# Loading one expert's weights piece by piece behind the streamed pieces, and the table rows later, at the seam of a fused three-layer kernel

## The chip, the cores and the metric

The kernel runs on one core of one Trainium2 chip. The metric is the device time of one execution in microseconds, and lower is better. Before the change, three runs took 1038.91 to 1043.51 us, with a median of 1040.13 us.

## What is computed

Three layers follow one another. The first is attention over 4 x 8 heads of 576 tokens, in which each row keeps its 32 largest scores. The second is a dense layer on 2304 tokens of width 512: `h = x @ w_in`, a gate, `@ w_out` (hidden width 2048). The third sends each token to one of 8 experts:

```python
logits = xn @ en.T / tau
expert_idx = np.argmax(logits, axis=1)
...
for e in range(E):
    mask = expert_idx == e
    h = np.maximum(x[mask] @ w1[e], 0.0)
    out[mask] = gate_w[mask, None] * (h @ w2[e])
```

`w1[e]` is 512 x 1024 and `w2[e]` 1024 x 512, both 2 MB. All is in 32-bit floats; a product is made of three matmuls on a high and a low part of each factor (high x high, high x low, low x high).

## The kernel before

Five engines work from lists of their own, in the order in which the program names their instructions: PE (matmuls and transposes), DVE and ACT (vector and scalar work), POOL (vector work and the indirect DMAs), and SP, which issues the plain DMAs. The order is written out by hand, and each engine keeps it: an instruction that waits holds back all that stand behind it on its engine.

The tokens come in groups of 128. Attention hands pairs of groups to the dense layer, which works in 8 steps (`q`, here also `n`) per pair. A step has a first half (`s1`, 24 matmuls of 256 columns, line 602) and a second half (`s2`, 12 matmuls of 512 columns, line 637), and the second half of a step runs after the first half of the next one. The high parts of the dense weights stay on the chip. The low parts are written to DRAM once and streamed back for every pair, one piece of 512 KB (`lo`) per half step; each of the two streams has two buffers, so SP can issue a piece when the half step two before has freed its buffer (line 286).

The last pair of groups (16 and 17, `finals`) has nothing left to overlap with but the third layer, and the seam between them is where the change lies. The function `behind(n, k)` is called four times in each of the last 8 steps, `k` = 0 in the middle of the first half, 1 after it, 2 and 3 after each part of the second half. It places these things there:
- `place()` writes the rows of a group's tokens into a table in DRAM (`tbl`), sorted by expert, by an indirect DMA on POOL (line 729).
- `expert(r)` reads the number of the expert with rank `r` (by size) into a register of SP (line 801). `load_ids` reads that expert's rows of the table (`idt`, line 806), `get` gathers up to 128 token rows (`xg`) by them on POOL (line 976), and `turn_in` transposes a block of them on PE (line 987) and splits it into a high and a low part on ACT and DVE.
- `load1` and `load2` load an expert's `w1` and `w2` in four pieces of 512 KB each (lines 811 and 820); `split_1` and `split_2` make the high part of a piece on ACT (line 824) and the low part on DVE (line 825).

After the loop the two final groups are scored: transposed, multiplied with the experts' embeddings (lines 1105 and 1114), their experts chosen on DVE (`choose`), ranked (`rank`: two small matmuls on PE, then positions on DVE) and placed. The rows of the table that belong to blocks 2 and 3 of the first expert can be read only then. Around these stand the first expert's own matmuls on its blocks 0 and 1 (`hidden`, line 917; `second`, line 951). From then on the eight experts follow one another, and each one's weights and rows are loaded while the one before is computed. `TURNS` is the order of the experts. The experts with rank 0 and 1 are called the first and the next expert below.

Of the kernel before, what the change touches and what calls it, by code (L numbers as in the profile page):

```python
# [20 lines left out]
DM, FF = 512, 2048  # L21
# [72 lines left out]
def layers(tc: tile.TileContext, qt, kt, v, w_in, w_out, embt, tau, w1, w2, out, y_dram, g_dram, tbl, lo_dram, flag, pools, consts):  # L94
# [704 lines left out]
    def expert(r):  # L799
        if r not in evs:  # L800
            evs[r] = nc.values_load(ordi[0:1, r:r + 1], engines=[ET.SP], min_val=0, max_val=E - 1)
            idts[r] = late["ids"].tile([128, 4, 2], I32, name=f"idt{r}")

    def load_ids(r, b0, b1):
        expert(r)
        nc.sync.dma_start(out=idts[r][:, b0:b1, :], in_=tbl[bass.ds(evs[r] * STRIDE + 128 * b0, 128 * (b1 - b0)), :].rearrange("(n p) t -> p n t", p=128))

    def load1(r):
        t = late["w1" if r == 0 else "wb"].tile([128, 4, F2], F32, tag="raw", name="a1")
        for k in range(4):  # L810
            nc.sync.dma_start(out=t[:, k, :], in_=w1r[:, bass.ds(evs[r], 1), k, :].rearrange("p o f -> p (o f)"))
        ws1[r] = t

    w2r = w2.rearrange("e (k p) d -> p e k d", p=128)
    ws2 = {}

    def load2(r):
        t = late["w1"].tile([128, 8, DM], F32, tag="raw", name="a2")
        for k in range(0, 8, 2):
            nc.sync.dma_start(out=t[:, k:k + 2, :], in_=w2r[:, bass.ds(evs[r], 1), k:k + 2, :].rearrange("p o k d -> p (o k) d"))  # L820
        ws2[r] = t

    def split(hi, lo, x):
        nc.scalar.copy(hi, x)  # L824
# [64 lines left out]
    if True:  # L889
# [17 lines left out]
        def hidden(r, f, c0, c1, half=None):  # L907
            xh_, xl_ = tok[r]
            h1, l1 = ws1[r]
            if r not in hs:  # L910
                hs[r] = [hp.tile([128, 8, CAPS[0]], F32R, tag=t, name=t) for t in ("hh", "hl")]
            if half != 1:
                xt_[f] = late["ph"].tile([128, 512], F32, tag="ph", name="ph2")[:, :c1 - c0]
            ph = xt_[f]
            for k in ((0, 1), (2, 3), (0, 1, 2, 3))[2 if half is None else half]:
                for n, (l, x) in enumerate(((h1, xh_), (h1, xl_), (l1, xh_))):
                    nc.tensor.matmul(ph, l[:, k, 128 * f:128 * f + 128], x[:, k, c0:c1], start=(k == 0 and n == 0), stop=(k == 3 and n == 2))

        def hidden_out(r, f, c0, c1):
            hh, hl = hs[r]  # L920
            ph = xt_.pop(f)
            nc.scalar.activation(hh[:, f, c0:c1], ph, AF.Relu)  # L922
            nc.vector.scalar_tensor_tensor(hl[:, f, c0:c1], ph, 0.0, hh[:, f, c0:c1].bitcast(F32), op0=ALU.max, op1=ALU.subtract)  # L923
# [18 lines left out]
        def second(r, b, fs_):  # L942
            hh, hl = hs[r]
            h2, l2 = ws2[r]
            n, o, m = b
            if (r, n) not in sums_:
                sums_[r, n] = po_.tile([128, DM], F32, tag="po", name="po2")
            po = sums_[r, n]
            for f in fs_:
                for i, (a, w) in enumerate(((hh, h2), (hl, h2), (hh, l2))):  # L950
                    nc.tensor.matmul(po[:m, :], a[:, f, o:o + m], w[:, f, :], start=(f == 0 and i == 0), stop=(f == 7 and i == 2))
# [21 lines left out]
        def get(r, b):  # L973
            n, o, m = b
            xg_[r, n] = xg = late["xg"].tile([128, DM], F32, tag="xg", name="xg")
            nc.gpsimd.indirect_dma_start(out=xg[:m, :], out_offset=None, in_=y_dram,
                                         in_offset=bass.IndirectOffsetOnAxis(ap=idts[r][:m, n, 0:1], axis=0))
# [13 lines left out]
        def split_1(r, k):  # L991
            if k == 0:
                ws1[r] = (ws1[r], [late["w1"].tile([128, 4, F2], F32R, tag=t, name=t) for t in ("h1", "l1")])
            a1, (h1, l1) = ws1[r]
            split(h1[:, k, :], l1[:, k, :], a1[:, k, :])
            if k == 3:
                ws1[r] = (h1, l1)

        def split_2(r, k):
            if k == 0:  # L1000
                ws2[r] = (ws2[r], [wb.tile([128, 8, DM], F32R, tag=t, name=t, bufs=2) for t in ("h2", "l2")])
            a2, (h2, l2) = ws2[r]
            split(h2[:, 2 * k:2 * k + 2, :], l2[:, 2 * k:2 * k + 2, :], a2[:, 2 * k:2 * k + 2, :])
            if k == 3:
                ws2[r] = (h2, l2)

        def gate_part(k):
            if k == 0:
                for t, g in finals:
                    sq = gp.tile([128, DM], F32, tag="ob", name="sql")  # L1010
                    nc.scalar.activation(sq, t, AF.Square, accum_out=ss_all[:, g:g + 1])
            elif k == 1:
                late["nrm"] = nrm = fs.tile([128, NG], F32, tag="nrm", name="nrm")
                nc.scalar.activation(nrm, ss_all, AF.Sqrt)
                nc.vector.tensor_scalar(nrm, nrm, 1e-6, None, op0=ALU.add)
                nc.vector.reciprocal(nrm, nrm)
                df = late["df"]
                nc.vector.tensor_tensor(df, df, nrm.unsqueeze(2).broadcast_to([128, NG, E]), op=ALU.mult)
                nc.scalar.activation(df, df, AF.Exp)
            elif k == 2:  # L1020
                late["gt"] = gt = fs.tile([128, NG], F32, tag="gt", name="gt")
                nc.vector.tensor_reduce(gt, late["df"], axis=AX.X, op=ALU.add)
                nc.vector.tensor_scalar(gt, gt, 1e-9, None, op0=ALU.add)
                nc.vector.reciprocal(gt, gt)
            else:
                pg = half_a()
                nc.tensor.transpose(pg[:NG, :128], late["gt"], ident)
                gts = fs.tile([NG, 128], F32, tag="df", name="gts")
                nc.vector.tensor_copy(gts, pg[:NG, :128])
                nc.sync.dma_start(out=g_dram[0:NT, :].rearrange("(g p) o -> g (p o)", p=128), in_=gts)  # L1030
# [5 lines left out]
        def behind(n, k):  # L1036
            n -= base
            if (n, k) == (0, 1):
                place()
            elif (n, k) == (0, 3):  # L1040
                side.popleft()()
            elif (n, k) == (1, 0):
                side.popleft()()
            elif (n, k) == (1, 1):
                side.popleft()()
                place()
            elif (n, k) == (1, 3):
                side.popleft()()
                choose()
            elif (n, k) == (2, 0):  # L1050
                rank()
                place()
            elif (n, k) == (2, 1):
                place()
            elif (n, k) == (3, 1):
                expert(0)
                load1(0)
            elif (n, k) == (3, 3):
                load_ids(0, 0, 2)
            elif (n, k) == (4, 0):  # L1060
                for x in bl[0][:2]:
                    get(0, x)
            elif (n, k) == (6, 0):
                turn_in(0, bl[0][0])
            elif (n, k) == (6, 2):
                turn_in(0, bl[0][1])
            elif (n, k) == (6, 3):
                load2(0)
                expert(1)
            if (n, k) in ((4, 1), (4, 3), (5, 1), (5, 3)):  # L1070
                split_1(0, ((4, 1), (4, 3), (5, 1), (5, 3)).index((n, k)))

        with tc.manual_schedule():
            at.close()
# [24 lines left out]
            load1(1)  # L1099
            C = (0, 256)  # L1100
            yts = []
            for o, (t, g) in enumerate(finals):
                pp = px.tile([128, 4, 128], F32, tag="px", name="pxt")
                for k in range(4):
                    nc.tensor.transpose(pp[:, k, :], t[:, 128 * k:128 * k + 128], ident)
                yts.append(gp.tile([128, 4, 128], F32, tag="ob", name="ytl"))
                nc.scalar.copy(yts[o], pp)
                hidden(0, 0, *C, o)
            split_2(0, 0)
            hidden_out(0, 0, *C)  # L1110
            p2 = half_a()
            for o, (t, g) in enumerate(finals):
# [2 lines left out]
                scored[0] += 1  # L1115
            nc.vector.tensor_copy(l_all[:, NG - 2:NG, :], p2[:, :2 * E].rearrange("p (g e) -> p g e", e=E))
            choose()
            hidden(0, 1, *C)
            hidden_out(0, 1, *C)
            hidden(0, 2, *C, 0)  # L1120
            rank()
            place()
# [7 lines left out]
            for f in (3, 4, 5):  # L1130
                split_2(0, f - 2)
                first(0, f, *C)
            load_ids(1, 0, 4)
            load2(1)
            for r in TURNS[2:]:
                load_ids(r, 0, 4)
            for n in (2, 3):
                get(0, bl[0][n])
            gate_part(0)
            for f in (6, 7):  # L1140
                first(0, f, *C)
# [4 lines left out]
            turn_in(0, bl[0][2])  # L1146
            get(1, bl[1][0])
            gate_part(3)
            second(0, bl[0][1], range(4, 7))
            turn_in(0, bl[0][3])  # L1150
            get(1, bl[1][1])
# [136 lines left out]
```

## Time and profile before

| what | before |
|---|---|
| median of three runs | 1040.13 us |
| the profiled execution | 1039.81 us |
| its span, first to last instruction | 1038.0 us |
| TensorE (PE) busy | 956.5 us, 92% |
| VectorE (DVE) busy | 759.7 us, 73% |
| ScalarE (ACT) busy | 712.4 us, 69% |
| GpSimd (POOL) busy | 632.0 us, 61% |
| mean granted clock of TensorE | 0.968 |
| DMA, mean over the span | 174 GB/s |

The profile shows one execution. Times are counted from the span's start; the span leaves out 1.8 us of the execution's own time. "Idle before" is what an engine waited in front of an instruction, with the engine or DMA that ended the wait. The granted clock is a share of TensorE's full 2.4 GHz. Attention ends at about 700 us, the seam lies between 740 and 820 us, and the experts take the rest.

### The profile page before, as it was taken

What the parts mean: (1) busy time and instruction counts of PE and PEld (TensorE: products, weight loads), DVE (VectorE), ACT (ScalarE), POOL (GpSimd) and SP (SyncE); (2) the same over time, 40 slices, a digit from 0 to 9 for tenths busy, and PEclk for the clock granted to TensorE, in tenths of its full rate; (3) what the DMA queues carried; (4) which work ended last, traced back from release to release, by engine and by line L of the source; (5) the groups of instructions that cost most, each with busy time, mean ns of one, the idle gap of its engine ahead of it and who ended that gap; (6) DMA issues with size and microseconds to landing.
All of it is one profiled execution on the core that took longest, in us unless ns stands there. A gap on an engine that the chain in (4) does not pass through costs nothing. (4 is left out here: it accounts for less than half of the span.)

```text
span 1038.0 us, 20808 instructions
## 1 busy us (share of the span) xinstructions
PE 956.5 (92%) x7196; PEld 834.8 (80%) x7196; DVE 759.7 (73%) x2349; ACT 712.4 (69%) x1437; POOL 632.0 (61%) x786
## 2 busy tenths in 40 slices
PE   2666788999999999999999999999989999999997
PEld 1443576889999999999999987889878888888986
DVE  7999999998988988888888888861233454455551
ACT  4899798897788788798787877773334454455551
POOL 4789899877768877678876765763331353223220
PEclk9966799999999999999999999999999999999999
DMA  5555677743455654267564375556684465544620
GB/s 195 178 160 183 220 245 249 230 154 128 133 172 157 201 164 137 88 186 236 127 184 138 101 253 179 157 192 196 170 274 164 127 230 209 203 137 160 236 95 22
DMA packets 85905, 180.96 MB, mean 174 GB/s; under 512 B 16157, under 2 KB 30640, under 8 KB 85791
## 3 DMA queue, kind: packets, MB, share of 16 engines
q1 hardware_dynamic: 81231, 169.68, 50.8%
q0 software_dynamic: 4416, 9.80, 3.0%
q8 instruction: 59, 0.97, 0.4%
q14 instruction: 55, 0.45, 0.1%
q10 hardware_dynamic: 144, 0.07, 0.0%
HBM read 157.41 MB, written 18.89 MB: 170 GB/s over the span
## 5 line engine op out<-in xcount | busy, mean ns | idle before, releaser
L487 POOL TENSOR_TENSOR s<-s,z 128x576 f32<-128x576 f32 x144 | 190.0, 1320 | 63.1 <-ACT z L483 62.5
L602 PE MATMUL bank_h<-xh,vh 128*128 128x256 f32 x576 | 171.4, 298 | 0.0
L602 PE MATMUL bank_h<-xl,vh 128*128 128x256 f32 x576 | 163.7, 284 | 0.0
L602 PE MATMUL bank_h<-xh,lo 128*128 128x256 f32 x576 | 163.5, 284 | 0.0
L469 DVE MAX8 A<-left 128x8 f32<-128x288 f32 (+1 forms) x288 | 159.7, 596 | 0.0
L520 PE MATMUL bank_t<-ident,s 128*128 128x128 f32 x648 | 107.8, 290 | 31.7 <-ACT pt L525 19.7
L525 ACT COPY pt<-bank_t 128x384 f32<-128x384 f32 x216 | 102.1, 481 | 37.0 <-PE bank_t L520 35.9
L520 PEld LDWEIGHTS bank_t<-ident,s 128*128 128x128 f32 x648 | 81.4, 148 | 53.9 <-ACT pt L525 22.8
L621 POOL TENSOR_TENSOR gl<-u,gh 128x512 fp32r<-128x512 f32 x72 | 92.9, 1290 | 47.6 <-ACT gh L618 44.4
L637 PE MATMUL y<-lo,gh 128*128 128x512 f32 x288 | 114.2, 397 | 4.8 <-DMA lo<-lo_dram 4.8
L441 ACT COPY s<-ps_sc 128x576 f32<-128x576 f32 x143 | 92.2, 645 | 38.1 <-PE ps_sc L430 13.9
L637 PE MATMUL y<-wh,gh 128*128 128x512 f32 x288 | 118.2, 410 | 0.0
L483 ACT ACTIVATE z<-s,nb 128x576 bf16<-128x576 f32 x144 | 112.6, 782 | 5.3 <-POOL nb L477 5.3
L637 PE MATMUL y<-wh,gl 128*128 128x512 f32 x288 | 113.8, 395 | 0.0
L493 ACT ACTIVATE s<-s,nb 128x576 f32<-128x576 f32 x144 | 113.4, 788 | 0.5 <-POOL s L487 0.5
L602 PEld LDWEIGHTS bank_h<-xl,vh 128*128 128x128 f32 x576 | 110.8, 192 | 0.3
L602 PEld LDWEIGHTS bank_h<-xh,vh 128*128 128x128 f32 x576 | 110.8, 192 | 0.3
L602 PEld LDWEIGHTS bank_h<-xh,lo 128*128 128x128 f32 x576 | 110.6, 192 | 0.0
L970 POOL DMA_INDIRECT out_dram<-ob,idt x21 | 24.9, 1185 | 139.0 <-ACT ob L963 95.4
L610 ACT ACTIVATE u<-bank_h,half 128x512 f32<-128x512 f32 x72 | 50.0, 694 | 69.2 <-PE bank_h L602 67.7
L825 DVE TENSOR_TENSOR l<-a,h 128x1024 fp32r<-128x1024 f32 x64 | 76.3, 1230 | 26.8 <-ACT h L824 21.8
L923 DVE SCALAR_TENSOR_TENSOR hl<-ph,hh 128x256 fp32r<-128x256 f32 (+5 forms) x72 | 31.7, 440 | 87.2 <-ACT hh L922 85.9
(248 smaller groups left out, 2679.5 us busy)
## 6 DMA issues: line engine op xcount, KB each, us to landing
lo<-lo_dram SPq DMA_DIRECT2D x144, 512.0 KB
a<-in_moe_w_dram SPq DMA_DIRECT2D x64, 512.0 KB
vt<-in_v_dram SPq DMA_DIRECT2D x28, 320.0 KB
w<-in_moe_w_in_dram SPq DMA_DIRECT2D x16, 512.0 KB
w<-in_moe_w_out_dram SPq DMA_DIRECT2D x16, 512.0 KB
lo_dram<-wf SPq DMA_DIRECT2D x32, 256.0 KB
qraw<-in_q_dram SPq DMA_DIRECT2D x48, 128.0 KB
krs<-in_k_dram SPq DMA_DIRECT2D x16, 288.0 KB
```

Source lines behind the costliest of these rows:

```text
L441: nc.scalar.copy(sbuf[i % NS][:, :, HS * g:HS * g + HS], ps_[i][:, :, :HS])
L469: nc.vector.max(A[:, n, 8 * r:8 * r + 8], src[:, n, :w])
L483: nc.scalar.activation(zb_[n], tile_of(i, n), AF.Relu, bias=sel[i][1][:, n, 1:2], scale=-BIG)
L487: nc.gpsimd.tensor_tensor(s, s, zb_[n], op=ALU.subtract)
L493: nc.scalar.activation(s, s, AF.Exp, bias=sel[i][1][:, n, 0:1], scale=SCALE, accum_out=sums[i][:, n:n + 1])
L520: nc.tensor.transpose(pp[:, 128 * k:128 * k + 128], e[:, 128 * (3 * c + k):128 * (3 * c + k) + 128], ident)
L525: nc.scalar.copy(pts[i][:, 3 * c:3 * c + 3, :].rearrange("p k n -> p (k n)"), tb_.pop((i, c))[:, :384])
L602: nc.tensor.matmul(ph[:, a, :], w, x[:, k, :], start=(k == 0 and n == 0), stop=(k == 3 and n == 2))
L610: nc.scalar.activation(u, state[q, "h"], AF.Relu, bias=half, scale=1.0 / 6.0)
L621: nc.gpsimd.tensor_tensor(state[q][1], state.pop((q, "u")).rearrange("p (a n) -> p a n", a=2), state[q][0].bitcast(F32), op=ALU.subtract)
L637: nc.tensor.matmul(state["y"][o], x[:, a, c], w, start=(f == 0 and n == 0), stop=(f == 15 and n == 2))
L825: nc.vector.tensor_tensor(lo, x, hi.bitcast(F32), op=ALU.subtract)
```

## The change

Seven things move; nothing is added or taken away:
- the four pieces of the first expert's `w1`, all issued at step (3, 1), are issued one by one at (3, 3), (4, 1), (4, 3) and (5, 1);
- their splits move from (4, 1), (4, 3), (5, 1), (5, 3) to (4, 3), (5, 1), (5, 3), (6, 1);
- the first two blocks' table rows and gathers move from (3, 3) and (4, 0) to (5, 3), and their `turn_in` from (6, 0) and (6, 2) to (7, 0) and (7, 2);
- the first expert's `w2` moves from (6, 3) to (7, 3);
- after the loop, `hidden` of step 0 stands ahead of the final groups' transposes, and `hidden` of step 1 in the gaps where step 0 stood;
- the first split of `w2` moves from before the choice to after it;
- the gathers of blocks 2 and 3, and the other experts' table rows, come ahead of the next expert's `w2`, which is loaded in two halves.

```diff
-    def load1(r):
-        t = late["w1" if r == 0 else "wb"].tile([128, 4, F2], F32, tag="raw", name="a1")
-        for k in range(4):
-            nc.sync.dma_start(out=t[:, k, :], in_=w1r[:, bass.ds(evs[r], 1), k, :].rearrange("p o f -> p (o f)"))
-        ws1[r] = t
+    raw1, raw2 = {}, {}
+
+    def load1(r, parts=range(4)):
+        if 0 in parts:
+            ws1[r] = raw1[r] = late["w1" if r == 0 else "wb"].tile([128, 4, F2], F32, tag="raw", name="a1")
+        for k in parts:
+            nc.sync.dma_start(out=raw1[r][:, k, :], in_=w1r[:, bass.ds(evs[r], 1), k, :].rearrange("p o f -> p (o f)"))
...
-            elif (n, k) == (3, 1):
-                expert(0)
-                load1(0)
-            elif (n, k) == (3, 3):
+            elif (n, k) == (5, 3):
                 load_ids(0, 0, 2)
-            elif (n, k) == (4, 0):
                 for x in bl[0][:2]:
                     get(0, x)
-            elif (n, k) == (6, 0):
+            elif (n, k) == (7, 0):
                 turn_in(0, bl[0][0])
-            elif (n, k) == (6, 2):
+            elif (n, k) == (7, 2):
                 turn_in(0, bl[0][1])
-            elif (n, k) == (6, 3):
+            elif (n, k) == (7, 3):
+                expert(1)
                 load2(0)
-                expert(1)
-            if (n, k) in ((4, 1), (4, 3), (5, 1), (5, 3)):
-                split_1(0, ((4, 1), (4, 3), (5, 1), (5, 3)).index((n, k)))
+            if (n, k) == (3, 3):
+                expert(0)
+            if (n, k) in PARTS1:
+                load1(0, (PARTS1.index((n, k)),))
+            if (n, k) in SPLITS1:
+                split_1(0, SPLITS1.index((n, k)))
+
+        PARTS1 = ((3, 3), (4, 1), (4, 3), (5, 1))
+        SPLITS1 = ((4, 3), (5, 1), (5, 3), (6, 1))
...
             yts = []
+            hidden(0, 0, *C)
             for o, (t, g) in enumerate(finals):
...
                 nc.scalar.copy(yts[o], pp)
-                hidden(0, 0, *C, o)
-            split_2(0, 0)
+                hidden(0, 1, *C, o)
             hidden_out(0, 0, *C)
...
             choose()
-            hidden(0, 1, *C)
             hidden_out(0, 1, *C)
+            split_2(0, 0)
             hidden(0, 2, *C, 0)
             rank()
...
-            load_ids(1, 0, 4)
-            load2(1)
-            for r in TURNS[2:]:
-                load_ids(r, 0, 4)
             for n in (2, 3):
                 get(0, bl[0][n])
+            for r in TURNS[1:]:
+                load_ids(r, 0, 4)
+            load2(1, (0, 1))
...
             gate_part(3)
+            load2(1, (2, 3))
             second(0, bl[0][1], range(4, 7))
```

`load2` is changed as `load1` is.

On SP, around the first expert's `w1` (tiles: `lo0` and `lo1` the streamed pieces of the two halves, `a1` a weight piece, `idt0` the table rows, `ordi` the expert numbers). Before:

```order
L286 DMA lo0_9788<-lo_dram0_60 128x1024
L801 TENSOR_LOAD ordi_90
...
L811 DMA a1_9808<-in_moe2_w1_dram 128x1024
...
L286 DMA lo1_9825<-lo_dram1_61 128x1024
L806 ISA
L806 DMA idt0_9807<-tbl_59 128x2x2
L286 DMA lo0_9856<-lo_dram0_60 128x1024
L286 DMA lo1_9881<-lo_dram1_61 128x1024
```

The row of `a1` stands there four times, one behind the other. Now:

```order
L286 DMA lo0_9788<-lo_dram0_60 128x1024
L286 DMA lo1_9809<-lo_dram1_61 128x1024
L801 TENSOR_LOAD ordi_90
...
L814 DMA a1_9822<-in_moe2_w1_dram 128x1024
L286 DMA lo0_9848<-lo_dram0_60 128x1024
L814 ISA
L814 DMA a1_9822<-in_moe2_w1_dram 128x1024
L286 DMA lo1_9870<-lo_dram1_61 128x1024
...
L286 DMA lo1_9925<-lo_dram1_61 128x1024
L806 ISA
L806 DMA idt0_9821<-tbl_59 128x2x2
```

The `lo1` piece that stood behind the expert number and all four weight pieces now stands ahead of them, and each `a1` piece has a `lo` piece behind it. The read of the table rows moved behind the last of them.

On DVE, around the choice for the final groups (`l_all` the scores, `picks` the choice, `pos` to `rows` the positions in the table, `l2` the low part of a weight piece, `hl` an expert's hidden values). Before, from the first split of `w2` on:

```order
L825 TENSOR_TENSOR l2_10137<-a2_9997,h2_10136 128x1024
L923 SCALAR_TENSOR_TENSOR hl_10115<-ph2_10116,hh_10114 128x256
L1116 COPY l_all_88<-bank_a_120 128x16
...
L702 TENSOR_TENSOR picks_83<-eqs_10152,first_10155 128x16
L923 SCALAR_TENSOR_TENSOR hl_10115<-ph2_10160,hh_10114 128x256
L714 TENSOR_TENSOR pos_10184<-bank_a_120,ebase_78 128x16
```

Now:

```order
L925 SCALAR_TENSOR_TENSOR hl_10108<-ph2_10109,hh_10107 128x256
L1121 COPY l_all_88<-bank_a_120 128x16
...
L702 TENSOR_TENSOR picks_83<-eqs_10161,first_10164 128x16
L925 SCALAR_TENSOR_TENSOR hl_10108<-ph2_10129,hh_10107 128x256
L827 TENSOR_TENSOR l2_10172<-a2_10053,h2_10171 128x1024
L714 TENSOR_TENSOR pos_10184<-bank_a_120,ebase_78 128x16
```

The subtraction for the first piece of `w2` moved from before the scores' copy to between the choice and the positions.

On SP, behind the table rows of blocks 2 and 3 (`idt1` to `idt5` the other experts' rows, `a2` a piece of the next expert's `w2`). Before:

```order
L806 DMA idt0_9807<-tbl_59 128x2x2
L806 ISA
L806 DMA idt1_10012<-tbl_59 128x4x2
L820 ISA
L820 DMA a2_10255<-in_moe2_w2_dram 128x2x512
...
L801 TENSOR_LOAD ordi_90
L801 ISA x2
L806 ISA
L806 DMA idt2_10270<-tbl_59 128x4x2
```

Now:

```order
L806 DMA idt0_9821<-tbl_59 128x2x2
L806 ISA
L806 DMA idt1_10052<-tbl_59 128x4x2
L801 TENSOR_LOAD ordi_90
L801 ISA x2
L806 ISA
L806 DMA idt2_10269<-tbl_59 128x4x2
...
L806 DMA idt5_10329<-tbl_59 128x4x2
L823 ISA
L823 DMA a2_10331<-in_moe2_w2_dram 128x2x512
```

All four `a2` pieces stood ahead of the six row loads that need an expert number; now the first two stand behind them, and the other two behind the write of the gates.

## Rows read from the trace of the kernel before

**Rows 1.** The page: busy time and share of the span of each engine.
```profile
PE 956.5 (92%) x7196; PEld 834.8 (80%) x7196; DVE 759.7 (73%) x2349; ACT 712.4 (69%) x1437; POOL 632.0 (61%) x786
```

**Rows 2.** Waits of PE, 680 to 1038 us: sum, times, longest.
```profile
PE y L637 <- DMA lo<-lo_dram: 4.4, 2, 3.0
PE pxt L987 <- DMA xg<-y_dram,idt: 1.9, 1, 1.9
...
PE pxt L1105 <- ACT ysl L648: 0.7, 1, 0.7
```

**Rows 3.** Windows: length; busy time of each engine; granted clock, DMA share, GB/s.
```profile
757.30:760.24 2.94, 0.00 (x0) 0.00 (x1) 0.69 (x1) 2.13 (x4) 0.00 (x0) 1.00 0.94 282
760.24:764.45 4.21, 4.21 (x11) 3.34 (x12) 2.36 (x2) 0.92 (x1) 3.49 (x3) 0.59 0.90 330
...
782.21:786.70 4.49, 3.02 (x13) 1.99 (x11) 0.00 (x0) 0.59 (x1) 1.00 (x1) 1.00 0.12 48
...
810.98:813.07 2.09, 0.17 (x1) 0.03 (x1) 0.00 (x0) 0.00 (x0) 0.00 (x0) 1.00 1.14 236
```

**Rows 4.** PE's timeline at the seam: start, duration, line, operation.
```profile
756.89 0.39 PE L637 MATMUL y<-wh,gh 128*128 128x512 f32 x1
...
767.32 0.40 PE L637 MATMUL y<-wh,gh 128*128 128x512 f32 x1
...
770.07 0.28 PE L602 MATMUL bank_h<-xh,vh 128*128 128x256 f32 x1
...
787.53 0.65 PE L1105 MATMUL pxt<-ident,ysl 128*128 128x128 f32 x4 [0.68 <-ACT ysl L648]
...
793.81 0.18 PE L711 MATMUL bank_a<-picks,tri 128*128 128x16 bf16 x1
```

**Rows 5.** SP's timeline at the seam: start and length of issues, line, transfer.
```profile
747.48 2.20 SPq L811 DMA_DIRECT2D a<-in_moe_w_dram  x4
749.78 0.58 SPq L286 DMA_DIRECT2D lo<-lo_dram  x1
756.74 0.38 SPq L806 DMA_DIRECT2D idt<-tbl  x1
...
773.32 3.00 SPq L820 DMA_DIRECT2D a<-in_moe_w_dram  x4
...
801.80 0.97 SPq L806 DMA_DIRECT2D idt<-tbl  x2
803.02 2.08 SPq L820 DMA_DIRECT2D a<-in_moe_w_dram  x4
805.91 9.19 SPq L806 DMA_DIRECT2D idt<-tbl  x6
```

**Rows 6.** DVE's timeline around the choice for the final groups.
```profile
790.94 1.22 DVE L825 TENSOR_TENSOR l<-a,h 128x1024 fp32r<-128x1024 f32 x1 [9.79 <-ACT h L824]
...
792.41 0.17 DVE L1116 COPY l_all<-bank_a 128x16 f32<-128x16 f32 x1
...
794.78 0.17 DVE L718 CAST rows<-de 128x2 int32<-128x2 f32 x1
```

**Rows 7.** POOL's timeline: two gathers, the second with no weights beside it.
```profile
805.20 0.97 POOL L976 DMA_INDIRECT xg<-y_dram,idt  x1 [6.53 <-issue]
...
881.01 1.05 POOL L976 DMA_INDIRECT xg<-y_dram,idt  x1 [0.55 <-PE pxt L987]
```

**Rows 8.** DMA queues: 747.4 to 757, 757.21 to 764, 805.2 to 809, 809 to 813.1, 881 to 883.
```profile
DMA packets 733, 2.59 MB, mean 269 GB/s; under 512 B 105, under 2 KB 105, under 8 KB 732
...
DMA packets 864, 2.15 MB, mean 317 GB/s; under 512 B 339, under 2 KB 339, under 8 KB 864
...
q1 hardware_dynamic: 625, 1.21, 92.2%
...
q0 software_dynamic: 185, 0.62, 53.3%
...
q0 software_dynamic: 43, 0.05, 12.5%
```

More of the change, by code (lines that the diff above doesn't have):

```diff
@@ L806, in load_ids, with load2 @@
         nc.sync.dma_start(out=idts[r][:, b0:b1, :], in_=tbl[bass.ds(evs[r] * STRIDE + 128 * b0, 128 * (b1 - b0)), :].rearrange("(n p) t -> p n t", p=128))
-    def load1(r):
-        t = late["w1" if r == 0 else "wb"].tile([128, 4, F2], F32, tag="raw", name="a1")
-        for k in range(4):
-            nc.sync.dma_start(out=t[:, k, :], in_=w1r[:, bass.ds(evs[r], 1), k, :].rearrange("p o f -> p (o f)"))
-        ws1[r] = t
+    raw1, raw2 = {}, {}
[4 more added lines that the diff above has]
+            nc.sync.dma_start(out=raw1[r][:, k, :], in_=w1r[:, bass.ds(evs[r], 1), k, :].rearrange("p o f -> p (o f)"))
     w2r = w2.rearrange("e (k p) d -> p e k d", p=128)
     ws2 = {}
[L817 to L821, printed above, removed]
+    def load2(r, parts=range(4)):
+        if 0 in parts:
+            ws2[r] = raw2[r] = late["w1"].tile([128, 8, DM], F32, tag="raw", name="a2")
+        for k in parts:
+            nc.sync.dma_start(out=raw2[r][:, 2 * k:2 * k + 2, :], in_=w2r[:, bass.ds(evs[r], 1), 2 * k:2 * k + 2, :].rearrange("p o k d -> p (o k) d"))
     def split(hi, lo, x):
```

## The prediction

> **What bounds the kernel now.** I read four views, in this order. First the page's busy line: TensorE (PE) is busy 92% of the span, 956.5 us of 1038.0 [rows 1], so the sum of its work sets the time, and a change that leaves its work alone can win only idle time in front of its instructions. Second, the waits of PE from 680 us to the end, the only part whose order the change moves: 4.4 us in two waits for a low piece of the streamed weights (`lo`), 1.9 us in one wait for gathered token rows (`xg`), 0.7 us for a copy by ACT [rows 2]. That is nearly everything there is to win. Third, the windows and PE's timeline around these waits, for what each really costs. Fourth, SP's timeline with the DMA queues, for why the data is late.
>
> *The first wait.* The block of twelve 512-column matmuls that begins at 756.89 stops after one matmul. PE is idle from 757.30 to 760.24, and the eleven that remain then run at a granted clock of 0.59 (1.2 GHz for most of it) until 764.45 [rows 3, 4]. The same block undisturbed runs from 767.32 to 770.07, 2.75 us [rows 4]. So this place costs 764.45 - 756.89 - 2.75 = 4.81 us, not 2.96. The cause stands on SP's timeline: four 512 KB weight pieces of the first expert are issued at 747.48, and the piece PE waits for goes out behind all four, at 749.78 [rows 5]. The DMA queues moved 2.59 MB in the 9.6 us from 747.4 [rows 8]; the piece is the last half megabyte of that, and PE had it at 760.24. Then SP stands until 756.74 for the table write that the row load needs [rows 5], holding back the pieces behind it.
>
> *The second wait.* The last such block takes 4.49 us from 782.21 to 786.70 instead of 2.75: 1.74 us [rows 3]. Same pattern: four pieces of the second weights at 773.32, and the last `lo` piece behind them [rows 5].
>
> *The third.* At 810.98 PE waits until 813.07, 2.09 us [rows 3], for rows that a gather on POOL fetches. The gather starts at 805.20 [rows 7]; SP had issued 2 MB of weights at 803.02 [rows 5]. From 805.2 to 809 the hardware queue moved 1.21 MB and the gathers' queue not one packet; all 185 of its packets lie between 809 and 813.1 [rows 8].
>
> **The change part by part.** It adds and removes no computation; DMAs, matmuls and vector instructions are the same, in another order. So each term is a wait.
>
> *Weight pieces one by one behind `lo` pieces; row load two steps later.* The `lo` piece of the first wait now goes to SP ahead of the expert number and ahead of every weight piece, and nothing needs it before 756.89. Later `lo` pieces have one 512 KB weight piece before them instead of four. Is there room? A `lo` piece may start when the block two before it has freed its buffer, three half steps of about 2.8 us ahead of its use, 8.4 us. In a half step two pieces, 1.05 MB, must pass: 373 GB/s. With the queue full the trace moved 317 GB/s from 757.21 to 764 and 269 GB/s from 747.4 to 757, the idle start included [rows 8]. At 317 a pair takes 3.3 us, so it slips 0.5 us per half step, 2.0 us over four; at 269, 1.1 and 4.4 us. The lead that is left is 8.4 less one pair (3.3) less some 2 us from issue to first bytes (the gather begun at 881.01 needed less), 3 us. At 317 nothing is late; at 269 the last piece is late by some 1.9 us. The term is -4.81 us, with -2.9 as its poor end. I take -4.81, since 317 is the row of pure streaming. The row load no longer meets an unfinished table write. The two gathers behind it start some 3 us later (756.74 to about 760 for the row load); their transposes move one step of 5.6 us later, and so have about 8 us, what the gather beside a stream of weights took (805.20 to 813.07). Casts and subtractions of the pieces move to later half steps on ACT and DVE, which are idle there for longer than one cast; the matmuls that need them come after 786.70. Cost 0.
>
> *Second weights behind the last piece.* The 1.74 us go, but the block's third matmul needs a low part from POOL whose subtraction in the trace of before ends at about the time the wait hid. A transposition that now stands in the block before (0.4 us) covers most of that. Term -1.67, between -1.1 and -1.74.
>
> *Finals.* From the end of the block at 786.70 to the rank matmul at 793.81 are 7.11 us, of which the first 0.83 are a wait for ACT's copy and the other 6.28 are PE's work [rows 3, 4]. Twelve expert matmuls now stand in that gap, and twelve more come before the score matmuls, so only six are left between the scores and the rank. Those six (half of a 512-column matmul each, 0.23/2, so 0.7 us) no longer cover DVE's choice: from the copy at 792.41 to the rank matmul at 793.81 it is 1.40 us [rows 4, 6]. New time: 6.28 - 0.7 + 0.1 + 1.40 = 7.1 us. The 0.83 us wait moves to the rank matmul: term 0, from -0.8 (no wait there) to +0.9.
>
> *Split ahead of the rank.* The order now puts a weight subtraction (1.22 us) on DVE between the choice and the positions; before, it stood ahead of the copy [rows 6]. So the rows, written at 794.78 + 0.17, come 1.0 us later, and with them POOL's table writes, the row load (801.80) and the gather, to about 806.2 on before's clock. Nobody on PE waits for the positions themselves.
>
> *Gathers ahead of the weights.* On SP the six other row loads now stand before the next weights, and those are halved. A row load with its expert number took 1.2 us where it did not wait (803.02 + 2.08 to 805.91, and its issue), so the first half goes out at about 811 instead of 803, and the second after the gate write. The gather starts at 806.2 against an empty queue. A gather of that kind, begun at 881.01, had 43 packets through by 883 [rows 7, 8], and the rest within about 2 us. It lands at some 810 to 811, and PE comes at 810.98. Term: between -2.09 and, if the gather is as slow as before, +1.0 (that slowness with a later start). I take -1.8. The weights' first cast comes some 8 us after their new issue: no cost.
>
> **Sum.** -4.81 - 1.67 + 0 - 1.8 = -8.3 us. The profiled execution took 1039.81 us (span 1038.0); that gives 1031.5. The median of the runs of before is 1040.13, 0.3 us above the profiled one, so I say 1031.7. All best ends give -9.5, all poor ends -2.9 - 1.1 + 0.9 + 1.0 = -2.1.
>
> **The rivals.**
> *The gather's delay is its own.* Then putting the weights behind it brings nothing, and the later rows lengthen the wait to 3.1 us: -4.81 - 1.67 + 1.0 = -5.5, 1034.3 us. For it: the gathers and the weights use different queues. Against it: no packet for 3.8 us beside the stream, 43 within 2 us without one. The Trainium skill ("DMA: Bandwidth & Descriptors", section on queues, rings and completion order) says that each DMA engine takes turns between its queues packet by packet, which would let the gather through beside the weights. The trace agrees only from 809 on, when both queues move packets, and not in the 3.8 us before. Chance 0.16.
>
> *The stream is late in small doses.* At 269 GB/s one or two `lo` pieces are late, by 1.9 us each and with a slow clock behind one of them (1.45 us more, the excess of 760.24 to 764.45 over 2.76): 1033.6 to 1036.5. For it: the demand of 373 GB/s lies above both rates. Against it: only four half steps ask for it. Chance 0.13.
>
> *Slower: the interleaved stream collapses.* If pieces from two places of memory pass at 150 GB/s together, each pair takes 7.0 us instead of 2.8; over four, 16.7 us of slip less 5.6 of lead, 11.1 us of waits, with a slow stretch after two of them, 2.9 us: 1031.5 + 14.0 = 1045.5. It decides against the change below some 170 GB/s (14.2 of slip less 5.6 is 8.6). For it: nothing but that no row shows this mixture. Against it: 317 GB/s in the stretch where `lo` pieces, row loads and gathers ran together. Chance 0.03.
>
> *The waits were not what the order sets*, and other late data takes their place one step on: no change, 1038 to 1041. Chance 0.06.
>
> **How the numbers follow.** The forecast has 0.62. A measurement of this kernel tells about 0.5%, 5.2 us, from no change, so faster means below 1034.9. The forecast and half of the first two rivals lie there, and some of it is lost to runs at the border: faster 0.80, same 0.17, slower 0.03. The range runs from 1029.5 (all best ends, less a run as quick as the quickest of before, 1.2 us under its median) to 1036.5, which takes in the first two rivals and leaves out the last two.
>
> **What would show it.** In the profile after: PE's waits list no `lo` of a microsecond or more, and the clock stays at 1.0 there; the block between the streamed part and the rank still has a wait, now of 0.8 to 0.9 us at the rank matmul for DVE; the gather begins about 19.5 us after the last streamed block and its wait is below 0.5 us. A wait for `lo` with rates near 270 GB/s beside it would speak for the second rival, a wait of 2 to 3 us for `xg` for the first. The forecast is wrong if the time is above 1034.9.

## The result, and the profile after

The changed kernel took 1031.59 us (median of six runs, 1030.42 to 1034.5) beside 1040.25 us for the kernel before (median of six, the three runs given ahead among them): a ratio of 0.9913, 95% interval 0.989 to 0.9935. The profiled execution took 1031.51 us, its span is 1029.7 us. That is the predicted time (1031.7); the way to it is not quite the predicted one.

The page's busy line and the waits of PE from 680 us on answer to [rows 1, 2]: PE does the same work, and no wait for `lo` or `xg` is left.

```profile
PE 956.3 (93%) x7196; PEld 834.7 (81%) x7196; DVE 757.7 (74%) x2349; ACT 712.6 (69%) x1437; POOL 633.6 (62%) x786
```

```profile
PE bank_a L711 <- DVE picks L702: 0.5, 1, 0.5
PE ph L919 <- DVE ordi L788: 0.4, 1, 0.4
PE ph L919 <- DVE hl L925: 0.4, 2, 0.2
PE y L637 <- POOL gl L621: 0.3, 1, 0.3
PE bank_a L751 <- DVE pos L714: 0.3, 1, 0.3
```

Windows of the changed kernel: the block of the first wait, the last streamed block, the stretch to the rank matmul, the 3.44 us behind the rank, the rest up to the transposes of block 2 (columns as in [rows 3]).

```profile
755.88:758.63 2.75, 2.75 (x14) 2.26 (x13) 0.69 (x1) 1.68 (x3) 0.29 (x1) 1.00 1.00 313
776.39:779.76 3.37, 3.06 (x13) 2.17 (x12) 0.69 (x1) 0.59 (x2) 0.89 (x1) 1.00 0.93 338
779.76:786.63 6.87, 6.38 (x55) 6.26 (x54) 1.51 (x8) 3.25 (x6) 0.00 (x0) 1.00 0.85 286
786.63:790.07 3.44, 3.33 (x17) 3.25 (x16) 2.56 (x8) 1.32 (x2) 2.38 (x4) 0.52 0.51 204
790.07:805.14 15.07, 14.91 (x90) 13.07 (x90) 6.90 (x14) 8.12 (x15) 5.29 (x5) 1.00 0.30 50
```

The first block takes 2.75 us at full clock instead of 7.56; the last one 3.37 instead of 4.49 [rows 3]. New is the fourth line: behind the rank the granted clock is 0.52, which is 1.2 GHz for nearly all of the 3.44 us. PE's timeline shows what the last block and the rank wait for:

```profile
777.33 0.50 PE L637 MATMUL y<-wh,gl 128*128 128x512 f32 x1 [0.32 <-POOL gl L621]
...
783.48 1.85 PE L1119 MATMUL bank_a<-ent,ytl 128*128 128x8 f32 x16
...
786.63 0.17 PE L711 MATMUL bank_a<-picks,tri 128*128 128x16 bf16 x1 [0.50 <-DVE picks L702]
```

SP's timeline answers to [rows 5], and one line of the DMA queues (757 to 763 us) to the 317 GB/s of [rows 8]:

```profile
748.84 0.36 SPq L814 DMA_DIRECT2D a<-in_moe_w_dram  x1
750.46 0.32 SPq L286 DMA_DIRECT2D lo<-lo_dram  x1
...
759.17 0.39 SPq L806 DMA_DIRECT2D idt<-tbl  x1
761.70 8.46 SPq L286 DMA_DIRECT2D lo<-lo_dram  x3
772.07 2.89 SPq L823 DMA_DIRECT2D a<-in_moe_w_dram  x4
...
795.62 8.36 SPq L806 DMA_DIRECT2D idt<-tbl  x8
804.24 0.95 SPq L823 DMA_DIRECT2D a<-in_moe_w_dram  x2
```

```profile
DMA packets 683, 2.35 MB, mean 392 GB/s; under 512 B 109, under 2 KB 109, under 8 KB 683
```

The pieces alternate, the second weights start after the last `lo` issue (761.70 + 8.46), and the next weights go out at 804.24, long after the gather, which POOL starts at 799.33.

### The profile page after: what moved, and what is told of

It is laid out like the page before. It is cut to its first block, busy times and chain, and to the rows that moved or that the text cites. A ratio compares the mean times of both kernels' runs of the same rounds, so it can differ in the third digit from the quotient of the medians.

```text
span 1029.7 us, 20811 instructions
## 1 busy us (share of the span) xinstructions
PE 956.3 (93%) x7196; PEld 834.7 (81%) x7196; DVE 757.7 (74%) x2349; ACT 712.6 (69%) x1437; POOL 633.6 (62%) x786
## 5 line engine op out<-in xcount | busy, mean ns | idle before, releaser
L509 POOL TENSOR_SCALAR s<-s,sums 128x576 f32<-128x576 f32 x112 | 82.8, 751 | 21.1 <-DVE sums L500 20.0
L538 PE MATMUL bank_a<-pt,vt 128*64 128x128 f32 (+1 forms) x1600 | 94.2, 277 | 0.6 <-ACT pt L525 0.6
```

The costliest lines, as they stand in the source:

```text
L509: nc.gpsimd.tensor_scalar(x, x, rv[:, n:n + 1], 1.0, op0=ALU.mult, op1=ALU.mult)
L538: nc.tensor.matmul(av[64 * n:64 * n + 64, c0:c1], vt[:, k, 64 * n:64 * n + 64], pt[:, k + 5 * n if k < 4 else 4, c0:c1], start=(o == 0), s ...
```

## How the kernels are compared below

The intervals of the ratios below are 1.5 to 2.9 us wide to either side, and a reason can be seen in the profiles: the matmul of `order` (line 751, which counts for the ranking of the experts), ahead of everything that the change moves, starts at 744.10 us before, at 743.10 us after, and between 741.83 and 747.81 us in the other profiles. So each kernel is read from that matmul on, in three stretches of PE's timeline: **A** to the end of the streamed blocks (0.23 us, the spacing, behind the start of the last such matmul), **B** from there to the second rank matmul (line 711), **C** from there to the transposes of block 2. What follows C takes 224.4 to 225.9 us in all of them. Each row has one profile, so its A, B and C are of one execution. The ratio is to runs of the kernel before on the same chip: 1039.3 us for the four that have one part alone, 1040.26 us for the four that begin with "changed,", 1039.22 us for "the same again", "both of these" and "more cover".

| kernel | A | B | C | sum | median, us | ratio to before (95%) |
|---|---|---|---|---|---|---|
| before | 42.60 | 7.11 | 19.26 | 68.97 | 1040.25 | |
| changed | 36.66 | 6.87 | 18.51 | 62.04 | 1031.59 | 0.989 to 0.9935 |
| the same again | 36.66 | 6.88 | 18.55 | 62.09 | 1031.66 | 0.9912 to 0.9947 |
| w1 pieces alone | 43.92 | 7.11 | 18.90 | 69.93 | 1041.91 | 1.001 to 1.0039 |
| second weights alone | 41.32 | 7.13 | 18.45 | 66.90 | 1038.40 | 0.9979 to 1.0008 |
| both of these | 36.66 | 7.11 | 19.34 | 63.11 | 1032.28 | 0.9913 to 0.9946 |
| tail alone | 40.92 | 7.11 | 17.17 | 65.20 | 1038.91 | 0.9973 to 1.001 |
| finals alone | 43.25 | 6.88 | 20.46 | 70.59 | 1041.17 | 1.0008 to 1.0042 |
| changed, w1 in a burst | 38.61 | 6.87 | 18.50 | 63.98 | 1032.82 | 0.989 to 0.9944 |
| changed, rows early | 38.88 | 6.87 | 17.06 | 62.81 | 1032.58 | 0.9899 to 0.9954 |
| changed, finals as before | 36.65 | 7.12 | 17.17 | 60.94 | 1030.22 | 0.9877 to 0.9922 |
| changed, cover at the rank | 36.67 | 6.92 | 17.56 | 61.15 | 1031.34 | 0.9895 to 0.9947 |
| more cover in three places | 36.05 | 6.93 | 16.35 | 59.33 | 1027.29 | 0.9866 to 0.99 |

A alone differs by 2.3 us between the three profiles with the old stream (before, tail alone, finals alone): their late pieces are late by differing amounts. Where the new stream has no late piece (changed, the same again, both of these, finals as before, cover at the rank) it differs by 0.02 us.

## Experiments

**The w1 pieces alone.**

```diff
-            elif (n, k) == (7, 3):
-                expert(1)
-                load2(0)
+            elif (n, k) == (6, 3):
+                load2(0)
+                expert(1)
```

(beside the changed kernel; finals and tail as before the change)

> The kernel before with the first part alone: the first expert's w1 pieces one by one behind streamed pieces, their splits, the row load and the two gathers later; the second weights, the finals and the tail stay as before. Theory (a streamed piece is late only because of what was issued ahead of it, and each part acts by itself): the first wait goes whole, 4.8 us, the block takes 2.75 us at full clock; the last block (wait for a streamed piece) and the wait for the gather stay as before; 1035.4 us. Rival (other late data takes the place): the last block's wait grows, since four weight pieces now end only two steps ahead of the second weights; less than 3.5 us is won, 1036.8 us or more.

The rival won, and by more than it said: nothing is gained. The first wait is gone, as in the changed kernel, but the last block now waits 6.19 us. PE's timeline, SP's timeline and SP's waits (760 to 790 us) of this kernel:

```profile
785.58 0.80 PE L637 MATMUL y<-lo,gh 128*128 128x512 f32 x1 [6.19 <-DMA lo<-lo_dram]
```

```profile
774.61 2.12 SPq L823 DMA_DIRECT2D a<-in_moe_w_dram  x4
777.46 0.35 SPq L286 DMA_DIRECT2D lo<-lo_dram  x1
```

```profile
SPq L823 <- DVE l L827: 7.2, 1, 7.2
```

SP stands 7.2 us in front of the first `a2` piece until DVE's last split of `w1` ends: `a1` and `a2` have the same buffer (tag `raw` of one pool), and the change splits the last piece at (6, 1) instead of (5, 3), which on DVE is behind the work for one dense step more. The last `lo` piece stands behind `a2`, and PE has it 8 us after its issue. The same wait stood in the kernel before, only shorter (SP's waits, 740 to 830 us):

```profile
SPq L820 <- DVE l L825: 2.8, 1, 2.8
```

Counted from line 751's matmul (745.69 in this profile, 744.10 before), `a2` goes out 28.9 us later here and 29.2 us later before [rows 5]: PE came 4.8 us sooner, the data did not. The runs are 2.6 us slower than before (1039.3 us on that chip).

**The second weights alone.** Before, with `load2(0)` and `expert(1)` at (7, 3).

> The kernel before with one thing moved: the second weights of the first expert go behind the last streamed piece. Theory: the last block's wait for the streamed piece goes, but the wait for the low part that POOL makes, which it hid, shows in its place, with no transposition ahead of it 0.9 us at most: a gain of 0.9 to 1.2 us, 1039.1 us; the first wait and the gather's wait stay. Rival (the later second weights come late themselves): ACT waits for the first piece ahead of the scores and PE with it; no gain, 1040.2 us or more.

The last block goes as the theory had it: it (782.72 to 786.18) takes 3.46 us instead of 4.49, 1.03 less, and what it waits for is the low part:

```profile
783.78 0.50 PE L637 MATMUL y<-wh,gl 128*128 128x512 f32 x1 [0.45 <-POOL gl L621]
```

The first wait stays. The wait for the gather was 1.1 us instead of 1.9; why it shrank was not tried. The runs (1038.40 beside 1039.3 us) can't tell this kernel from the one before.

**Both together.** Before, with the pieces and the second weights; finals and tail as before.

> The kernel before with the weight pieces one by one and the second weights behind the last streamed piece together; finals and tail as before. Theory (with the pieces alone the second weights waited for the last w1 split to free their buffer, and held the last streamed piece back behind them; once that piece is ahead of them the two parts add up): no wait for a streamed piece, the stretch from the last order matmul to the end of the streamed blocks takes 36.7 us instead of 42.6, the wait for the gather stays at 1 to 2 us: 1034 us, 5 to 6.5 us better than before. Rival (the streamed piece of the last block is late for lack of bandwidth, whatever goes out ahead of it): a wait of 2 us or more is left in the last block, 1036 us or more.

A is 36.66 us, the changed kernel's to the hundredth, and the wait for the gather is 2.0 us. Its median is 1032.28 us beside 1039.22 for the kernel before. Beside the one profile of before, the two parts alone gave +1.32 and -1.28 us in A, together -5.94; beside the other two profiles with the old stream the pair gives -4.3 and -6.6. The gain belongs to the pair.

**The pieces in a burst.** The changed kernel with

```diff
-            if (n, k) in PARTS1:
-                load1(0, (PARTS1.index((n, k)),))
+            if (n, k) == (3, 3):
+                load1(0)
```

> The changed kernel with all four w1 pieces issued at once at (3, 3), behind the same streamed piece as its first one. Theory (each streamed piece may have only one weight piece ahead of it): the streamed piece behind the four lands 10 to 13 us after the first of them goes out, against 9.8 us until PE needs it, so PE waits 0.5 to 3 us, with a slow clock behind a long wait: 1032 to 1036 us. Rival (only the place counts: one streamed piece more ahead of the weights is enough): no wait, 1031.6 us.

SP's and PE's timeline of this kernel:

```profile
751.29 2.22 SPq L814 DMA_DIRECT2D a<-in_moe_w_dram  x4
753.62 7.76 SPq L286 DMA_DIRECT2D lo<-lo_dram  x4
```

```profile
763.20 0.38 PE L602 MATMUL bank_h<-xh,lo 128*128 128x256 f32 x1 [1.72 <-DMA lo<-lo_dram]
```

Its window behind the wait:

```profile
763.20:766.30 3.10, 3.10 (x24) 3.06 (x25) 0.00 (x0) 0.17 (x1) 0.00 (x0) 1.00 0.64 240
```

One wait of 1.72 us, with full clock behind it; A grows by 1.95 us. So, by one profile of each, the place behind one more `lo` piece, with the second weights behind the last, brings some two thirds of the gain in A and the one-by-one order the last third. The runs (1029.93 to 1037.1) can't tell it from the changed kernel; the profile can.

**The table rows early.** The changed kernel with `load_ids(0, 0, 2)` at (3, 3) again.

> The changed kernel with the row load of the first two blocks put back to (3, 3), ahead of the weight pieces; the gathers stay at (5, 3). Theory (SP stands at the row load until the table is written, some 7 us, and holds back the pieces behind it): the streamed piece that is issued at 750.5 us now goes out at 756 us and lands some 3 us after PE needs it; a wait of 2 to 3 us, with a slow clock behind it: 1034 to 1037 us. Rival (the lead of the stream hides SP's standing): 1031.6 us.

SP's timeline and waits (748 to 765 us), and PE's timeline:

```profile
759.38 0.41 SPq L806 DMA_DIRECT2D idt<-tbl  x1
760.04 0.35 SPq L814 DMA_DIRECT2D a<-in_moe_w_dram  x1
760.50 0.37 SPq L286 DMA_DIRECT2D lo<-lo_dram  x1
```

```profile
SPq L806 <- DMA tbl<-ids,rows: 5.9, 1, 5.9
```

```profile
765.34 0.39 PE L602 MATMUL bank_h<-xh,lo 128*128 128x256 f32 x1 [1.59 <-DMA lo<-lo_dram]
```

The place is right, the wait smaller than expected: SP stands 5.9 us, and the lead of the stream hides all but 1.59 us of it. A grows by 2.22 us, so some 2 of the 5.9 us need the row load moved. The runs (1032.58 us) can't tell this kernel from the changed one.

**The tail alone.** Before, with the gathers and row loads ahead of the next expert's weights.

> The kernel before with the tail alone: gathers of blocks 2 and 3 and the other table rows ahead of the next expert's second weights, these in two halves; the rest as before. Theory (the gather was held up by the weights' stream): the gather that starts near 805 moves its first packets within 2 us instead of after 3.8 us, and the wait for it, 2.1 us, goes; 1038.1 us. Rival (the delay is the gather's own): the wait stays within 0.5 us of 2.1 us, 1040.2 us. Both waits for streamed pieces stay.

C falls from 19.26 to 17.17 us, 2.09 less, the idle time of [rows 3]; PE no longer waits for `xg`. POOL's timeline, and the gathers' queue from 805.95 to 808 and from 808 to 810 us:

```profile
805.95 0.98 POOL L978 DMA_INDIRECT xg<-y_dram,idt  x1 [6.17 <-issue]
```

```profile
q0 software_dynamic: 7, 0.03, 6.3%
...
q0 software_dynamic: 124, 0.41, 58.6%
```

131 packets pass within 4.05 us of the gather's start, where there had been none in 3.8 us beside the weights [rows 8]. The first 2 us, with only row loads beside it, are the gather's own; the rest of the delay went with the weights. By the turn-taking between queues that the Trainium skill states ("DMA: Bandwidth & Descriptors", section on queues, rings and completion order) the gather would have got through there, so here the measurement decides. Whether its packets already stood in their queue beside the weights, no view shows; why they did not pass stays open. The median (1038.91 beside 1039.3 us) does not show the gain, since a run of this kernel varies by more.

**The finals alone.** Before, with the new order of the finals and of the first split.

> The kernel before with the finals' order alone: hidden of step 0 ahead of the transposes, step 1 in the gaps, the first split of the second weights behind the choice. Theory (the clock falls because PE waits at the rank right behind the small score matmuls): the 0.7 us wait for the copy goes, a wait of 0.5 us comes at the rank, the clock is near 0.5 for some 3 us behind it; the rows come 0.7 us later and the gather with them, so the wait for the gather, which hides the slow stretch, ends 0.5 us later than before: 1040.8 us. Rival (the slow stretch of the changed kernel came from its other parts): the clock is 1.0 behind the rank; the time is the same.

```profile
793.17:796.61 3.44, 3.33 (x17) 3.25 (x16) 2.56 (x8) 1.32 (x2) 2.38 (x4) 0.53 0.48 192
```

The window is the 3.44 us behind the rank: the slow stretch comes with this part. B is 0.23 us shorter, C 1.20 us longer. PE still waits for the gather (1.8 us), which hides the slow stretch; the gather starts 0.46 us later behind the streamed blocks than before (18.96 us beside 18.50), and its rows come another 0.5 us later.

**The changed kernel without it.** Finals and first split as before the change.

> The changed kernel with the order of the finals and of the first split as it was before the change. Theory (that reordering costs a slow clock behind the rank, and rows that come later): the 0.7 us wait for the copy is back, the rank has no wait, the clock is 1.0 behind it, the stretch from the rank to the transposes of block 2 takes 17.2 us instead of 18.5, and its rows are there in time: 1030.5 us, 1.1 us better than the changed kernel. Rival (the reordering is worth its 0.8 us and the slow stretch comes with either order): 1032.0 us.

The windows from the streamed blocks' end to the rank, of 3.44 us behind it, and the rest of C:

```profile
778.48:785.60 7.12, 6.44 (x55) 6.23 (x54) 2.60 (x9) 3.37 (x6) 0.11 (x1) 1.00 0.91 325
785.60:789.04 3.44, 3.44 (x31) 3.41 (x30) 2.37 (x7) 2.18 (x4) 2.12 (x5) 1.00 0.35 138
789.04:802.77 13.73, 13.32 (x77) 11.49 (x76) 6.31 (x14) 7.16 (x14) 4.31 (x4) 1.00 0.36 56
```

In the 3.44 us behind the rank 31 matmuls run, not 17. The sum is 1.10 us shorter than the changed kernel's, as expected: with the slow stretch, the reordering of the finals costs more than it brings. The runs agree in sign, but their intervals overlap.

**The changed kernel once more.**

> The changed kernel once more. Theory (the slow stretch behind the rank comes in most executions but not in all, since one kernel with the same order there kept its clock): either clock may show; the three stretches take 62.0 us with the slow stretch or 60.6 without it; 1031.6 us median. Rival (the slow stretch is fixed by the order): 62.0 us and a clock of 0.52 again.

The granted clock behind the rank was 0.56, and C 18.55 us, as the rival said. But with the same order there, the kernel with the early rows kept its clock through the same 0.49 us wait (793.56 is its rank):

```profile
793.56:797.00 3.44, 3.33 (x28) 3.24 (x28) 3.13 (x8) 2.04 (x4) 2.38 (x4) 1.00 0.44 173
```

Its C is 17.06 us. So of five profiles with this order (changed, again, finals alone, burst, early rows) four have the slow stretch; where it comes it costs about 1.45 us (18.51 less 17.06). In the eight profiles without a wait at the rank (the two kernels with cover below among them) the clock of these 3.44 us is 1.00 every time. So the wait goes with the slow stretch, but does not always bring it; what decides was not settled.

**Cover at the rank.** The changed kernel with

```diff
             hidden_out(0, 1, *C)
-            split_2(0, 0)
-            hidden(0, 2, *C, 0)
+            hidden(0, 2, *C)
             rank()
             place()
+            split_2(0, 0)
```

(and the second half of that `hidden` left out further down)

> The changed kernel with all twelve matmuls of hidden step 2 ahead of the rank instead of six, and the first split of the second weights behind the rank's positions. Theory (the slow clock comes from the idle time at the rank): no wait at the rank, the clock stays at 1.0, rows 1.0 us earlier, 1.0 to 1.5 us gained: 1030.3 us. Rival (the small score matmuls alone bring the clock down): the wait goes, 0.5 us, but the clock still falls for some 3 us behind the scores: 1031.2 us.

No wait at the rank, clock 1.00 behind it, 0.89 us less in the sum, where 1.0 to 1.5 were expected; the median, 1031.34 us, does not show it. The split now stands on DVE ahead of an `hl` that PE needs, and made a new wait, which is why C is 17.56 us and not less:

```profile
789.27 0.39 PE L919 MATMUL ph<-xh__9995,h 128*128 128x256 f32 x1 [1.01 <-DVE hl L925]
```

**More cover in three places.** That kernel, with the first split where DVE and ACT are idle, and the first transposition moved behind the last first half, where it covers POOL's low part:

```diff
-            elif (n, k) == (7, 0):
+            elif (n, k) == (7, 1):
                 turn_in(0, bl[0][0])
...
             hidden(0, 0, *C)
+            split_2(0, 0)
             for o, (t, g) in enumerate(finals):
...
             place()
-            split_2(0, 0)
```

> The changed kernel with more cover in three places: the first transposition stands behind the last first half instead of inside it, the first split of the second weights stands behind hidden of step 0, all of hidden step 2 stands ahead of the rank. Theory (the waits for gl, for picks and for hl are each set by what stands just ahead): the last block takes 2.85 to 3.0 us instead of 3.37, no wait at the rank and clock 1.0 behind it, hl waits below 0.5 us in sum; the three stretches from the last order matmul to the transposes of block 2 take 60.0 us in sum instead of 62.0; 1029.5 us. Rival (the gather's rows become the bound, since PE comes earlier): a wait for the gather of 0.5 us or more, 1030.5 us.

PE's waits from 730 us on, and the windows of B and of 3.44 us behind the rank:

```profile
PE ph L919 <- DVE ordi L788: 0.4, 1, 0.4
PE bank_a L751 <- DVE pos L714: 0.3, 1, 0.3
PE ph L919 <- DVE xl__10015 L991: 0.2, 1, 0.2
PE ph L919 <- DVE hl L925: 0.2, 1, 0.2
```

```profile
780.12:787.05 6.93, 6.93 (x61) 6.88 (x60) 2.79 (x9) 3.27 (x6) 0.03 (x1) 1.00 0.92 321
787.05:790.49 3.44, 3.40 (x30) 3.27 (x29) 2.87 (x9) 2.66 (x5) 2.12 (x5) 1.00 0.54 213
```

No wait for `gl`, `picks` or `xg` is left, and the last block takes 2.74 us (777.38 to 780.12). The sum is 59.33 us, 2.71 below the changed kernel's. Its median is 1027.29 us beside 1031.66 for the changed kernel on the same chip, and the two intervals (0.9866 to 0.99, 0.9912 to 0.9947) don't touch. The 1.7 us by which the medians differ more than the sums have no cause in these stretches.

## Why the prediction was right, and where its steps were not

- **What bounds the kernel: right.** PE's work stayed, and idle time in front of its instructions was what could be won.
- **First wait, -4.81: right in size, wrong as a term of its own.** The block went from 7.56 to 2.75 us, but the pieces alone only push the loss into the last block. The step that failed is "Casts and subtractions of the pieces move to later half steps [...] Cost 0": the last of them frees the buffer that SP needs for the second weights, and the last `lo` piece stood behind those on SP. In the pieces alone the wait in the last block grew to 6.19 us, from 1.47 before. The change's second part, which puts that piece first, hides it.
- **Last block, -1.67: it was -1.12**, near the poor end. The transposition was said to cover most of the low part's wait. One of the two transpositions did stand in the block ahead (774.56 us), but the chain that makes the low part was slower too: DVE's step began 1.15 us after ACT's (773.37, 774.52), and 0.79 us after it where the other transposition was moved out of the last first half (773.93, 774.72 in the kernel with more cover). Why it was slower was not settled.
- **Finals, 0: -0.24 in B.** The wait at the rank came where it was foreseen, but with 0.50 us, not 0.8 to 0.9. From the copy of the scores to the rank it is 1.26 us (785.37 to 786.63) and not 1.40: in the rows of before PE came to the rank after its own matmuls, with `picks` done at 793.63, so 1.40 was not DVE's time alone. **Not foreseen: the slow clock behind the wait, some 1.45 us, which the sum put at nothing.**
- **Gathers, -1.8: the mechanism right**, and -2.09 where it was tried alone. The gather started 19.57 us after the last streamed block (about 19.5 was said) and PE no longer waited. Of this gain C shows only 0.75 us; the slow stretch took the rest. One reading was off: of the 43 packets counted from 881 to 883 us, 32 pass by 881.6 and carry almost nothing; packets with data begin only behind 882.6 us, 1.6 us after that gather's start.
- **The sum.** The three stretches give -6.93 us, not -8.3. The profiled times differ by 8.30 because 1.00 us was won ahead of the first moved instruction, which is not the change's work, and 0.37 us behind C, which is less than the 1.5 us by which that part varies. With the clock held (C of 17.06) the sum would be -8.4 us. So the agreement to 0.1 us is partly luck, the size within 1.4 us is not: the medians gave 8.66 us the first time and 7.56 us the second (1039.22 less 1031.66).
- **Rivals.** The gather's own delay is refuted by the tail alone. Pieces late in small doses did not occur: the mixed stream passed at 392 GB/s where 317 had been assumed, and the collapse of the third rival is excluded by the same line. The demand of 373 GB/s lay above both rates only because these were read from stretches that hold more than the stream: the 269 GB/s begin with nearly idle queues (45 packets from 747.4 to 750 us), and of the 864 packets behind the 317 GB/s, which the prediction calls pure streaming, 339 are under 512 bytes [rows 8]. The burst of before, once under way, passed at 411 GB/s (752 to 757 us, line below). The second rival's price for a slow clock, 1.45 us, sets twelve matmuls against a stretch of eleven; eleven at 0.23 us leave 1.69 us. The fourth rival, that other late data takes the place one step on, is what the pieces alone showed; in the whole change the second part kept it out.

```profile
DMA packets 590, 2.05 MB, mean 411 GB/s; under 512 B 92, under 2 KB 92, under 8 KB 589
```

## What to carry to other kernels

When a step is moved later, ask which buffer its end frees, what transfer waits for that buffer, and which transfers stand behind that one on the queue: two edits that look independent can be worth little or nothing apart and 5.9 us together. Read the stretch that was edited in several profiles, from a matmul ahead of the edit, when the rest of the kernel varies by more than the edit is worth. Where a matmul waits for a chain of small vector instructions that hangs on small matmuls, put enough other matmuls between the two: half a microsecond of idle time there could cost 1.45 us more by the clock. And before a rate is used as what the queues can carry, see that its stretch holds neither a start from idle nor hundreds of tiny packets.

## What was not expected of the hardware

- The granted clock fell to 1.2 GHz behind an idle time of only 0.50 us, where 16 matmuls of 8 columns and six of 256 stood just ahead, in four of five profiles; in the fifth it stayed at 1.00 behind the same wait. An idle time of 0.68 us ahead of the final groups' transposes, behind full 512-column matmuls, did not (1.00 in the windows of the kernel with the old finals), nor did one of 1.72 us in the burst's kernel.
- Weight pieces and `lo` pieces issued in turn moved at 392 GB/s (757 to 763 us), about as fast as the burst of weight pieces in the kernel before, once it was under way (411 GB/s from 752 to 757 us).
- A gather's first packets of data come no sooner than 1.6 us after its start even without a weight stream beside it (behind 882.6 us for the one begun at 881.01 before the change; behind 807.6 us for the one begun at 805.95 in the tail alone).
